# A Fourier mixer with a gated feed-forward on one core: a planner counts its stores longer, holds back some of its first loads, plans anew, and puts the last half product in another bank

## The chip, the cores and the metric

The kernel runs on one core of one Trainium2 chip. The metric is the device time of one execution in microseconds (us), the median of the executions that were timed. The names of the engines in the profile are: PE (TensorE's matrix products), PEld (its weight loads, which overlap them), DVE (VectorE), ACT (ScalarE), POOL (GpSimd), SP (SyncE, which here issues nearly all transfers; SPq is that issuing). Every engine works through its own queue of instructions in order, and waits at the first one that isn't ready.

## The reference

x has 8192 rows of 448 numbers in f32. It is normalised row by row; one branch takes the Fourier transform along the 8192 rows, column by column, a small block-diagonal complex network on each frequency, and the inverse transform; the other is a gated feed-forward with 1792 hidden units. The silu of this branch times the transform branch is added to x.

```python
def reference(x, w1, b1, w2, b2, w_gate, w_up, w_down):
    xn = layernorm(x)                      # (8192, 448), eps 1e-5
    z = rfft(xn, along the 8192 rows)      # column by column; 4 blocks of 112 columns
    h = relu(z @ w1 + b1)                  # complex, real and imaginary part apart
    y = softshrink(h @ w2 + b2, 0.01)
    s = irfft(y, along the rows)
    f = (gelu(xn @ w_gate) * (xn @ w_up)) @ w_down      # 448 -> 1792 -> 448
    return x + s * silu(f)
```

## The kernel before, in words

**Arithmetic.** An f32 product is done as three f16 products (high by high, high by low, low by high). The large products of the feed-forward are also cut in 2 by 2 blocks and done as seven block products instead of eight, with sums of blocks made on DVE, ACT and POOL before and after. In the down projection these seven are `prod2(k, ...)` (line 1402) with k from 1 to 7; they add up in PSUM banks, and `add2` (line 1421) takes a bank into an SBUF tile `left` (the partial result of that quarter), scaled.

**Stages.** The opening (`begin`, `weights`, `begin1`) loads the first rows of x, normalises them and makes the first weights. Phase 1 runs over 16 chunks of 512 rows: layer norm, the first step of the transform, whose result `ysb` is stored to `t`, and units of the feed-forward, whose results `th` are stored to `prt` for the next pass. In the same stretch the block weights are made: sums of blocks (`wst`, `cb`) are cast to a high and a low f16 part (`wo`) on ACT and DVE or POOL, stored to the scratch tensors `wsp` (gate and up) and `dsp` (down), and loaded again from there when they are wanted. Phase 2 does the small network, group by group, between the units of the feed-forward. Phase 3 (`tiles3`, line 2077) does the inverse transform tile by tile (bank `bf`), multiplies with the gate (`g`), adds x and stores the output, again between units of the feed-forward.

**Banks and rings.** PSUM is used as four rings of two banks each, which the profile names `bx`, `by`, `bd` and `bf`. SBUF buffers are rings too. A product that opens a bank waits until DVE or ACT has read what stood there.

**The planner.** The order of the instructions isn't written out. A class `Pace` (line 47) runs all stages as tasks over a clock of its own: `issue` (line 137) finds from a table of costs when an instruction could start and when it would end, and a task goes on at that planned moment; the instructions come out in the order of the planned moments. So every instruction is recorded at one line (212). The planned clock has effect on the order alone; on the chip only semaphores decide. The table `STEPS` (line 41) sets, from a planned time on, a due-time width, what a load's planned end has added to it, how free an engine must be to be given a piece of work that either of two engines can do, and a factor on ACT's, DVE's and POOL's costs. In `issue` the end of a load after 100 us has such a term, and the end of a store has none. `END3` (line 2035) is the moment up to which phase 3's tiles are spread out.

**The end of the feed-forward.** In `down2` (line 1438), the last block product (k = 4) of the very last unit is done in halves of 224 columns, both in the same bank `x` (the profile's `bd`). After each half `last_half` (line 1527) adds this half to `left`, applies silu on ACT, multiplies by the transform's result, adds x and stores.

Of the kernel before, what the change touches and what calls it, by code (L numbers as in the profile page):

```python
# [32 lines left out]
DH = D // 2  # L33
# [6 lines left out]
EPS = 1e-5  # L40
STEPS = ((0, 2.75, 0.05, 1), (100, 2.5, 0.2, 1.03), (175, 3, 0.15, 0.98), (250, 2.75, 0.05, 1), (325, 2.5, 0.05, 1), (400, 2.75, 0.05, 1.04), (475, 2.75, 0.05, 1), (550, 3.5, 0.05, 1), (700, 2.75, 0.05, 1), (775, 2.5, 0.05, 0.985), (850, 2.75, 0.05, 0.97), (925, 2.75, 0.05, 1.06), (1150, 2.5, 0.05, 0.985), (1450, 3, 0.05, 1.02), (1525, 2.75, 0.05, 0.94), )
QUIET = 200.0
# [8 lines left out]
class Pace:  # L51
# [4 lines left out]
    def __init__(self):  # L56
        self.now, self.last, self.n, self.heap = 0.0, 0.0, 0, []
        self.free, self.seen, self.dma = {"SP": 0.7, "ACT": 0.7, "DVE": 0.7, "POOL": 0.7, "PE": 1.0}, {}, 1.75
        self.port = {"DVE": [], "POOL": []}
# [77 lines left out]
    def issue(self, e, op, out, ins, run):  # L137
        outs, ins, start = self.start(e, out, ins)
        if e == "SP" or op == "dma_start":
            size = (outs or ins)[0].nbytes()  # L140
            self.dma = max(self.dma, start) + size / (320e3 if start > 10.0 else 400e3)
            if start < 10.0:
                self.free[e] = start + 0.46
                end = self.dma + 0.9
            elif op == "dma_start_transpose":
                self.free[e] = start + 1.15 + size / 380e3
                end = max(self.free[e] + 2.6, self.dma + 1.5)
            else:
                self.free[e] = start + 0.5
                end = max(start + 2.2 + size / 240e3, self.dma + 1.5) + (self.step(start)[1] if outs and start > 100.0 else 0.0)  # L150
        else:
# [248 lines left out]
def afno_geglu_kernel(ctx, tc, x, gu, wd, mlp, b1, b2, c_m, c_mt, c_small, out):  # L400
# [1004 lines left out]
    def prod2(k, p, i, h, bank_, j0, j1, first=False, last=False, halves=(0, 1)):  # L1405
        (e, c), r = PROD2[k]
        for j in range(j0, j1):
# [6 lines left out]
            for t in halves:  # L1414
                for n, (s, v) in enumerate(((0, 0), (0, 1), (1, 0))):
                    T.matmul(bank_[:, DH * t:DH * t + DH], w[s][:, 128 * t:128 * t + 128], right(7 * j + r, v),
                             start=first and j == 0 and t == 0 and n == 0,
                             stop=last and j == PF[p][1] // 2 - 1 and t == 1 and n == 2, skip_group_check=True)
            yield pe()
# [18 lines left out]
    def down2(p, i, h, last):  # L1438
# [22 lines left out]
        def tail(mid=None):  # L1461
# [19 lines left out]
            tf = yield from TH.get()  # L1481
            for t in range(2):
                yield from prod2(4, p, i, h, x, 0, n, last=True, halves=(t,))
                pace.spawn(last_half(i, QS[3], x, tf, t), pace.last)

# [40 lines left out]

    def last_half(i, qq, b, tf, a):

        v = slice(a, a + 1)
        q, s4 = EV["ptb", i, qq][:, v], blk(state["last"], *qq)[:, v]  # L1530
        x4 = EV["lgt", i, qq[0]][-1][:, v, DH * qq[1]:DH * qq[1] + DH]
        th = tf.rearrange("p (a d) -> p a d", a=2)[:, v]
        V.scalar_tensor_tensor(q, part(b, 128, 2, DH)[:, v], cB[1], q, op0=ALU.mult, op1=ALU.add)
        yield
        S.activation(th, q, AF.Silu, scale=2.0)
# [636 lines left out]
    def begin():  # L2172
# [13 lines left out]
        Q.dma_start(w[:, 0:8 * 128], gu[0][:, 0:8 * 128])  # L2186
        for a in (1, 3):
            Q.dma_start(x4[:, a, :], xv[:, a, :])
        first = []
# [12 lines left out]
        S.activation(fb[:, 4:5], mhalf[:, 0:1], AF.Gelu_apprx_tanh)  # L2202
        S.copy(identf, ident)
        banks = []
        for R in (BF, BF, BD):
# [281 lines left out]
```

## Time and profile before

| | |
|---|---|
| median of 3 executions | 1764.88 us (1763.42 to 1767.83) |
| the profiled execution | 1765.09 us, its span 1763.3 us |
| PE busy | 1744.9 us, 99% of the span |
| DVE, ACT, POOL busy | 1420.1, 1089.9, 606.7 us |
| granted TensorE clock, mean | 0.997 |
| instructions | 41411, of them 16608 matrix products |

The view of the span in 40 slices shows where PE is not full: in the first slice, the opening, and in the last.

```profile
PE   8999999999999999999999999999999999999998
DVE  7868678887888888667877877888888888788888
ACT  6557666666666765556776767667676676333334
```

Each digit is the busy share of one fortieth of the span (44 us) in tenths, and 9 stands for 90% or more. To read such a kernel, the idle time of PE is what can be won or lost, as long as the number of products stays the same; the views that name what each idle stretch of PE waited for are the ones that matter.

### The profile page before, as it was taken

To read this page: it belongs to the slowest core of one execution; us is meant where nothing else is said; L and a number is where in the kernel's file an instruction comes from. 1 tells how busy PE (TensorE), PEld (TensorE's weight loads), DVE (VectorE), ACT (ScalarE), POOL (GpSimd) and SP (SyncE) were. 2 spreads that over 40 slices of the span, in tenths; PEclk is the share of its full clock that TensorE was granted. 3 is DMA by queue.
4 is the path that set the end of the run, shared out by engine and by line. 5 is a ranking of instruction groups with operands and counts; after the bars stand their busy time and mean duration, and the time that the engine had idled before them with its cause. 6 is when DMAs were issued, how large, how long until landed. Compare 5 with 4: busy or idle time off the path is not lost.

```text
span 1763.3 us, 41411 instructions
## 1 busy us (share of the span) xinstructions
PE 1744.9 (99%) x16608; PEld 1510.6 (86%) x16608; DVE 1420.1 (81%) x2551; ACT 1089.9 (62%) x2146; POOL 606.7 (34%) x737
## 2 busy tenths in 40 slices
PE   8999999999999999999999999999999999999998
PEld 4447678899988988999999999999999999888887
DVE  7868678887888888667877877888888888788888
ACT  6557666666666765556776767667676676333334
POOL 1144333665656665311322323223322232111111
PEclk8999999999999999999999999999999999999999
DMA  6365777667575663222345744443425544999995
GB/s 239 114 169 167 224 209 216 200 182 197 152 203 184 187 193 98 73 69 75 78 148 137 188 109 109 122 107 86 112 85 122 120 93 101 271 313 306 283 313 212
DMA packets 358465, 289.44 MB, mean 164 GB/s; under 512 B 235296, under 2 KB 327200, under 8 KB 358272
## 3 DMA queue, kind: packets, MB, share of 16 engines
q1 hardware_dynamic: 358128, 286.76, 57.3%
q8 instruction: 130, 2.13, 0.5%
q14 instruction: 63, 0.52, 0.1%
q10 hardware_dynamic: 144, 0.03, 0.0%
HBM read 131.44 MB, written 106.15 MB: 135 GB/s over the span
## 4 chain that ended last, share of the span: by engine, by line
PE 92%; DVE 5%; DMA 1%; issue 1%; ACT 1%; SPq 0%; POOL 0%; DVEq 0%; ACTq 0%
PE bx L212 30%; PE by L212 24%; PE bd L212 21%; PE bf L212 17%; DVE u L212 1%; DVE gl L212 1%; DMA wsp<-wo 0%; DVE st L212 0%; DVE th L212 0%; DVE h L212 0%; DVE left L212 0%; DMA x<-in_x 0%; SPq L212 0%; DMA m<-c_m 0%; DMA wdn<-in_down 0%
## 5 line engine op out<-in xcount | busy, mean ns | idle before, releaser
L212 PEld LDWEIGHTS <-wt 128*128 128x128 f16 x9350 | 906.2, 98 | 163.0 <-issue 11.6
L212 PE MATMUL bx<-xta,wt 128*128 128x256 f16 (+1 forms) x2979 | 371.6, 276 | 0.7 <-DVE by L212 0.6
L212 PEld LDWEIGHTS <-h 128*128 128x128 f16 x2716 | 260.1, 98 | 37.1 <-issue 1.6
L212 PE MATMUL by<-xtb,wt 128*128 128x256 f16 x2080 | 256.2, 273 | 2.0 <-DVE by L212 2.0
L212 POOL TENSOR_TENSOR wt<-wt 128x256 f32<-128x256 f32 x93 | 77.2, 830 | 318.2 <-DVE wt L212 253.5
L212 PE MATMUL bd<-dw,h 128*128 128x224 f16 (+1 forms) x1272 | 172.0, 280 | 1.0 <-DVE left L212 1.0
L212 PE MATMUL by<-xta,wt 128*128 128x256 f16 (+1 forms) x1059 | 142.2, 281 | 1.2 <-ACT wt L212 0.8
L212 PE MATMUL bx<-xtb,wt 128*128 128x256 f16 x1040 | 130.5, 273 | 3.5 <-DVE v L212 3.4
L212 DVE TENSOR_TENSOR by<-bx,u 128x512 f32<-128x512 f32 x104 | 72.5, 697 | 61.8 <-PE bx L212 56.9
L212 PE MATMUL bx<-left,wt 128*128 128x256 f16 x864 | 105.1, 272 | 0.0
L212 ACT COPY u<-by 128x512 f32<-128x512 f32 x104 | 60.8, 584 | 70.0 <-PE by L212 69.6
L212 ACT ACTIVATE u<-by,fc 128x512 f32<-128x512 f32 (+1 forms) x118 | 73.4, 635 | 47.4 <-PE by L212 46.1
L212 PE MATMUL bd<-dw,wt 128*128 128x224 f16 (+1 forms) x816 | 98.9, 264 | 0.2 <-ACT th L212 0.2
L212 ACT COPY by<-bx 128x512 f32<-128x512 f32 x104 | 59.8, 575 | 52.0 <-PE bx L212 51.4
L212 ACT CAST h<-wt 128x512 f16<-128x512 f32 (+1 forms) x128 | 68.4, 536 | 33.2 <-DVE wt L212 24.8
L212 DVE TENSOR_TENSOR v<-bx,u 128x512 f32<-128x512 f32 x104 | 71.4, 686 | 20.2 <-PE bx L212 19.0
L212 PE MATMUL bd<-wt,h 128*128 128x224 f16 x696 | 84.9, 259 | 0.1
L212 PE MATMUL bf<-w2t,wn 112*128 112x112 f16 x1512 | 84.7, 213 | 0.0
L212 PEld LDWEIGHTS <-left 128*128 128x128 f16 x864 | 81.8, 98 | 1.7 <-issue 0.2
L212 DVE SCALAR_TENSOR_TENSOR left<-bd,ms,left 128x448 f32<-128x448 f32 (+1 forms) x97 | 65.1, 675 | 21.7 <-PE bd L212 20.8
L212 PEld LDWEIGHTS <-wn 112*128 112x128 f16 x1512 | 80.4, 98 | 0.9
L212 POOL TENSOR_TENSOR zs<-t,zs 112x256 f16<-112x256 f32 (+2 forms) x40 | 36.4, 909 | 124.5 <-ACT zs L212 124.4
(269 smaller groups left out, 3572.3 us busy)
## 6 DMA issues: line engine op xcount, KB each, us to landing
xts<-sx SPq DMA_DIRECT2D x32, 480.0 KB, 3.0
x<-in_x SPq DMA_DIRECT2D x17, 896.0 KB, 6.2
t<-ysb SPq DMA_DIRECT2D x64, 224.0 KB, 3.2
prt<-th SPq DMA_DIRECT2D x64, 224.0 KB, 2.5
left<-prt SPq DMA_DIRECT2D x64, 224.0 KB, 3.9
u<-t SPq DMA_DIRECT2D x32, 448.0 KB, 6.0
x<-in_x SPq DMA_DIRECT2D x32, 448.0 KB, 6.6
y<-t SPq DMA_DIRECT2D x30, 448.0 KB, 3.6
```

Source lines behind the costliest of these rows:

```text
L212: return self.pace.issue(self.name, kind, out, ins, lambda: fn(out, *args, **kw))
```

## The change

It has five parts.

1. `STEPS` is replaced: 11 entries in the place of 15, with other numbers.
2. The planner's costs change: the first transfer counts from 2.05 us in the place of 1.75, transfers of the first 10 us count at 250 KB/us in the place of 400 with 0.65 after it in the place of 0.9, and the end of every store after 100 us has 1.5 us added. Loads keep their term from `STEPS`.
3. In `begin` the loads of the second and fourth row block of x (a = 1, 3) come after a `yield 3.1`, and what follows them after a `yield 3.5`; `weights()` and `load_m(0)` are spawned at 3.15 and 3.2 in the place of 0.1 and 0.2, the tasks behind them start at 3.4 in the place of 0.3, and `begin1` at 27 in the place of 23.
4. The last block product: its first half goes to the bank `x` as before, then the whole bank is added to `left` (`add2`). Its second half opens a new bank of the ring `bx` and is added to the second half of `left` by the new function `add_half`. `last_half` waits for these and no longer adds itself.
5. All of it is planned anew, so that the order moves on every engine.

```diff
-STEPS = ((0, 2.75, 0.05, 1), (100, 2.5, 0.2, 1.03), ...
+STEPS = ((0, 2.75, 0.05, 1), (100, 3.25, 0.05, 1), (300, 2.75, 0.05, 1), (400, 3.25, 0.05, 1), ...
...
-        ... "PE": 1.0}, {}, 1.75
+        ... "PE": 1.0}, {}, 2.05
...
-            self.dma = max(self.dma, start) + size / (320e3 if start > 10.0 else 400e3)
+            self.dma = max(self.dma, start) + size / (320e3 if start > 10.0 else 250e3)
...
-                end = self.dma + 0.9
+                end = self.dma + 0.65
...
-                end = max(...) + (self.step(start)[1] if outs and start > 100.0 else 0.0)
+                end = max(...) + ((self.step(start)[1] if outs else 1.5) if start > 100.0 else 0.0)
...
     def prod2(k, p, i, h, bank_, j0, j1, first=False, last=False, halves=(0, 1)):
-                             start=first and j == 0 and t == 0 and n == 0,
-                             stop=last and j == PF[p][1] // 2 - 1 and t == 1 and n == 2, skip_group_check=True)
+                             start=first and j == 0 and t == halves[0] and n == 0,
+                             stop=last and j == PF[p][1] // 2 - 1 and t == halves[-1] and n == 2, skip_group_check=True)
...
             tf = yield from TH.get()
-            for t in range(2):
-                yield from prod2(4, p, i, h, x, 0, n, last=True, halves=(t,))
-                pace.spawn(last_half(i, QS[3], x, tf, t), pace.last)
+            yield from prod2(4, p, i, h, x, 0, n, last=True, halves=(0,))
+            e = pace.spawn(add2(p, i, QS[3], x), pace.last)
+            pace.spawn(last_half(i, QS[3], e, tf, 0), pace.last)
+            w = yield from BX.get()
+            yield from prod2(4, p, i, h, w, 0, n, first=True, last=True, halves=(1,))
+            e = pace.spawn(add_half(i, QS[3], w, 1), pace.last)
+            pace.spawn(last_half(i, QS[3], e, tf, 1), pace.last)
...
-    def last_half(i, qq, b, tf, a):
+    def add_half(i, qq, b, a):
+        v = slice(a, a + 1)
+        q = EV["ptb", i, qq][:, v]
+        V.scalar_tensor_tensor(q, part(b, 128, 2, DH)[:, v], cB[1], q, op0=ALU.mult, op1=ALU.add)
+        yield
+
+    def last_half(i, qq, e, tf, a):
+        yield e
...
-        V.scalar_tensor_tensor(q, part(b, 128, 2, DH)[:, v], cB[1], q, op0=ALU.mult, op1=ALU.add)
-        yield
...
     def begin():
...
         Q.dma_start(w[:, 0:8 * 128], gu[0][:, 0:8 * 128])
-        for a in (1, 3):
-            Q.dma_start(x4[:, a, :], xv[:, a, :])
...
         S.copy(identf, ident)
+        yield 3.1
+        for a in (1, 3):
+            Q.dma_start(x4[:, a, :], xv[:, a, :])
+        yield 3.5
...
-        pace.spawn(load_m(0), 0.2)
         pace.spawn(begin())
-        pace.spawn(weights(), 0.1)
-        yield 0.3
+        pace.spawn(weights(), 3.15)
+        pace.spawn(load_m(0), 3.2)
+        yield 3.4
...
-        pace.spawn(begin1(), 23.0)
+        pace.spawn(begin1(), 27.0)
```

Three places of the new order follow. In the rows, a name before `<-` is the tile written, those after it the tiles read, then the shape; names are those of the profile with a buffer number.

**ACT, in phase 1, where a block of gate weights is cast to `wo` for the next store to `wsp`** (about 290 us into the trace of before; `gl` and `u` are the gate's and the up projection's results, taken out of the banks `bx` and `by`). Before:

```order
L212 COPY u_3340<-by 128x512
L212 ACTIVATE wo<-wst,fc 128x256
L212 ACTIVATE wo<-wst,fc 128x512
L212 ACTIVATE x_2696<-x_2696,st 128x448
L212 ACTIVATE gl<-bx,fc 128x512
L212 ACTIVATE u_3386<-by,fc 128x512
```

Now:

```order
L212 COPY u_3347<-by 128x512
L212 ACTIVATE x_2718<-x_2718,st 128x448 x2
L212 ACTIVATE gl<-bx,fc 128x512
L212 ACTIVATE u_3390<-by,fc 128x512
L212 CAST xs<-x_2718 128x2x448
L212 CAST h<-gl 128x256
L212 ACTIVATE ysb<-bf 128x2x224
L212 COPY sf<-x_2718 128x64
L212 ACTIVATE wo<-wst,fc 128x256
L212 ACTIVATE wo<-wst,fc 128x512
```

The two casts to `wo` stood ahead of the reads of `bx` and `by`; now they stand behind both, and behind four further pieces.

**SP's queue, about 200 us into the trace of before**, around a store of down weights (`dsp<-wo`). Before:

```order
L212 DMA t<-ysb 64x1792 x2
L212 DMA prt<-th 128x448 x2
L212 DMA dsp<-wo 256x1x1568
L212 DMA wdn<-in_down 128x2x448
L212 DMA x_2174<-in_x 128x1792
```

Now:

```order
L212 DMA t<-ysb 64x1792 x2
L212 DMA dsp<-wo 256x1x1568
L212 DMA wdn<-in_down 128x2x448
L212 DMA prt<-th 128x448 x2
L212 DMA x_2161<-in_x 128x1792
```

The store of `wo` stood behind the two stores of `th`; now it is issued ahead of them.

**DVE, its last pieces** (`left` reads a bank of the feed-forward, `g` one of the inverse transform; `th` and `g` are multiplied by the transform `s` or have `x` added, and are then stored). Before:

```order
L212 SCALAR_TENSOR_TENSOR left<-bd,ms,left 128x448
L212 TENSOR_TENSOR th<-th,x_25058 128x448
L212 SCALAR_TENSOR_TENSOR left<-bd,ms,left 128x224
L212 TENSOR_TENSOR th<-th,s_21907 128x448
L212 TENSOR_TENSOR th<-th,s_21907 128x224
L212 TENSOR_TENSOR th<-th,x_24887 128x448
L212 SCALAR_TENSOR_TENSOR left<-bd,ms,left 128x224
L212 TENSOR_TENSOR th<-th,x_25058 128x224
L212 TENSOR_TENSOR th<-th,s_21907 128x224
L212 TENSOR_TENSOR th<-th,x_25058 128x224
```

Now:

```order
L212 SCALAR_TENSOR_TENSOR left<-bd,ms,left 128x448
L212 TENSOR_TENSOR th<-th,s_22066 128x448
L212 SCALAR_TENSOR_TENSOR g_25273<-bf,ms,g_25273 128x448
L212 SCALAR_TENSOR_TENSOR left<-bx,ms,left 128x224
L212 TENSOR_TENSOR th<-th,s_22066 128x224
L212 TENSOR_TENSOR th<-th,x_25118 128x448
L212 TENSOR_TENSOR th<-th,x_25118 128x224
L212 TENSOR_TENSOR th<-th,s_22066 128x224
L212 SCALAR_TENSOR_TENSOR g_25273<-bf,ms,g_25273 128x448
L212 TENSOR_TENSOR th<-th,x_25118 128x224
L212 TENSOR_TENSOR th<-th,s_22066 128x448
L212 TENSOR_TENSOR th<-th,x_24866 128x448
```

The second half is read from `bx` in the place of `bd`, and a last tile of the inverse transform (`g_25273`) now falls in between. On PE its three products into `bf` are the very last, behind the second half in `bx`; POOL's last two rows are the additions of x to this `g`.

More of the change, by code (lines that the diff above doesn't have):

```diff
@@ L40 @@
 EPS = 1e-5
-STEPS = ((0, 2.75, 0.05, 1), (100, 2.5, 0.2, 1.03), (175, 3, 0.15, 0.98), (250, 2.75, 0.05, 1), (325, 2.5, 0.05, 1), (400, 2.75, 0.05, 1.04), (475, 2.75, 0.05, 1), (550, 3.5, 0.05, 1), (700, 2.75, 0.05, 1), (775, 2.5, 0.05, 0.985), (850, 2.75, 0.05, 0.97), (925, 2.75, 0.05, 1.06), (1150, 2.5, 0.05, 0.985), (1450, 3, 0.05, 1.02), (1525, 2.75, 0.05, 0.94), )
+STEPS = ((0, 2.75, 0.05, 1), (100, 3.25, 0.05, 1), (300, 2.75, 0.05, 1), (400, 3.25, 0.05, 1), (500, 2.75, 0.3, 1), (700, 2.5, 0.05, 0.985), (800, 2.75, 0.05, 1.03), (900, 2.5, 0.05, 0.985), (1000, 2.75, 0.05, 1), (1300, 2.75, 0.05, 1.06), (1500, 2.5, 0.05, 0.985), )
 QUIET = 200.0
@@ L57, in __init__ @@
         self.now, self.last, self.n, self.heap = 0.0, 0.0, 0, []
-        self.free, self.seen, self.dma = {"SP": 0.7, "ACT": 0.7, "DVE": 0.7, "POOL": 0.7, "PE": 1.0}, {}, 1.75
+        self.free, self.seen, self.dma = {"SP": 0.7, "ACT": 0.7, "DVE": 0.7, "POOL": 0.7, "PE": 1.0}, {}, 2.05
         self.port = {"DVE": [], "POOL": []}
@@ L149, in issue @@
                 self.free[e] = start + 0.5
-                end = max(start + 2.2 + size / 240e3, self.dma + 1.5) + (self.step(start)[1] if outs and start > 100.0 else 0.0)
+                end = max(start + 2.2 + size / 240e3, self.dma + 1.5) + ((self.step(start)[1] if outs else 1.5) if start > 100.0 else 0.0)
         else:
```

## The prediction

> **What bounds the kernel now.** I read the page's table of busy times and its chain of waits first.
>
> ```profile
> PE 1744.9 (99%) x16608; PEld 1510.6 (86%) x16608; DVE 1420.1 (81%) x2551; ACT 1089.9 (62%) x2146; POOL 606.7 (34%) x737
> PE 92%; DVE 5%; DMA 1%; issue 1%; ACT 1%; SPq 0%; POOL 0%; DVEq 0%; ACTq 0%
> ```
>
> PE is busy for 1744.9 of 1763.3 us, and the chain that ended last lies on it for 92%. The change keeps the number and the sizes of PE's products (16608 in both orders), so it can only move PE's idle time. The next view cuts the span into stages and gives PE's busy time in each: the first column is the stretch, the second its length, the third PE.
>
> ```profile
> 100.00:310.00 210.00, 205.17 (x1514) 147.36 (x1513) 156.04 (x286) 133.13 (x235) 75.27 (x109) 1.00 0.72 200
> 310.00:750.00 440.00, 437.84 (x4094) 394.62 (x4092) 363.51 (x671) 286.58 (x562) 250.48 (x316) 1.00 0.59 167
> 750.00:1650.00 900.00, 900.00 (x9553) 828.07 (x9551) 726.96 (x1270) 565.35 (x1146) 238.03 (x246) 1.00 0.52 140
> 1650.00:1757.20 107.20, 106.41 (x978) 94.43 (x977) 91.29 (x153) 41.94 (x73) 18.71 (x21) 1.00 0.87 276
> 1757.20:1763.30 6.10, 1.02 (x9) 0.77 (x8) 3.29 (x9) 0.96 (x3) 0.00 (x0) 0.95 0.37 127
> ```
>
> Length less busy gives PE's idle time: 4.83 us in the first row, 2.16, 0 and 0.79 in the next three, 5.08 in the last: 7.78 us over 1657 us of steady work, and a tail. That is small beside 1765 us, so this change can move the time by a few us either way. About 0.3% (5.3 us) is what a measurement of this kernel can tell from no change: the three runs shown lie up to 4.4 us apart. The band around the median is 1759.6 to 1770.2. The view of PE's waits names what the idle time waited for (us in all, times, longest), and that of the waits for DMA what stood behind it:
>
> ```profile
> PE bx L212 <- DVE v L212: 3.4, 2, 2.3
> PE bd L212 <- ACT xs L212: 2.9, 1, 2.9
> PE by L212 <- DVE by L212: 2.0, 2, 1.0
> PE bx L212 <- DVE gl L212: 1.4, 1, 1.4
> ACT wo L212 <- DMA wsp<-wo: 4.6, 2, 4.4
> ACT wo L212 <- DMA dsp<-wo: 1.9, 1, 1.9
> ```
>
> The longest is 2.3 us, and ACT waits there for a store, 4.4 us long. A store's end is what the change counts longer.
>
> **The store stall near 290 us.** The rows of the timeline (start, us, engine, operation, and in brackets the idle time ahead with its releaser):
>
> ```profile
> 288.10 0.36 SPq L212 DMA_DIRECT2D wsp<-wo  x1
> 295.71 1.12 ACT L212 ACTIVATE wo<-wst,fc 128x256 f16<-128x256 f32 x2 [4.36 <-DMA wsp<-wo]
> 297.39 0.67 ACT L212 ACTIVATE gl<-bx,fc 128x512 f32<-128x512 f32 x1
> 298.76 0.68 DVE L212 TENSOR_TENSOR v<-bx,u 128x512 f32<-128x512 f32 x1
> 299.49 1.25 PE L212 MATMUL bx<-xtb,wt 128*128 128x256 f16 x10 [2.30 <-DVE v L212]
> 306.00 0.88 PEld L212 LDWEIGHTS <-h 128*128 128x128 f16 x10 [0.40 <-DVE h L212]
> ```
>
> ACT wants to write `wo` again while the store of the old content is under way: issued at 288.10, let go just ahead of 295.71, 7.6 us. Behind it in ACT's queue stands `gl<-bx`, behind that DVE's `v<-bx`, and PE waits 2.30 us for that bank; a late `h` costs 0.40 more. In the new order both casts to `wo` stand behind `x` (twice), `gl<-bx`, `u<-by`, `xs`, `h`, `ysb` and `sf`. ACT was free for its wait at 295.71 - 4.36 = 291.35. The rows ahead of the casts now cost:
>
> ```profile
> 208.91 0.76 ACT L212 ACTIVATE x<-x,st 128x448 f32<-128x448 f32 x1
> L212 ACT ACTIVATE u<-by,fc 128x512 f32<-128x512 f32 (+1 forms) x118 | 73.4, 635 | 47.4 <-PE by L212 46.1
> 211.30 0.94 ACT L212 CAST xs<-x 128x896 f16<-128x896 f32 x1
> ```
>
> Two `x` of 0.76, `gl` 0.67, `u` 0.64 and `xs` 0.94 are 3.8 us, and with `h`, `ysb` and `sf`, taken at 1 us together as an estimate from the shapes of these rows, 4.8: ACT comes to `wo` at 296.2 or later, behind the landing. And if the store is still late, the bank reads are already done. So the 2.30 and the 0.40 go, **-2.7 us**; both ends: 0 if the store is itself issued 2 us later or more, -2.7 otherwise.
>
> **The store stall near 209 us** is alike, with a store to `dsp`:
>
> ```profile
> 201.42 1.40 SPq L212 DMA_DIRECT2D prt<-th  x2
> 202.91 0.56 SPq L212 DMA_DIRECT2D dsp<-wo x1
> 208.62 0.38 ACT L212 CAST wo<-wst 128x224 f16<-128x224 f32 x1 [1.85 <-DMA dsp<-wo]
> 210.92 1.25 PE L212 MATMUL by<-xtb,wt 128*128 128x256 f16 x10 [1.04 <-DVE by L212]
> ```
>
> ACT waits 1.85 us for it; `u<-by` and DVE's `by` are queued behind it, and PE waits 1.04. The store now goes ahead of the two `prt<-th`, which keep SP's queue for 1.40 us and wait for `th`. With 1.40 of the 1.85 gone, 0.45 is left on ACT, less than the 1.85 - 1.04 = 0.81 that the work already queued on PE covers. **-1.0 us**; the other end is 0.
>
> **The rest of the idle time** in phase 1, phase 2 and 3 is 7.78 - 2.3 - 0.4 - 1.0 = 4.1 us, in places where DVE or ACT comes a little late at a bank; all orders have them, and planning anew draws them afresh. The view of waits shows two more `bx` waits, of 1.1 (the other of 3.4) and 1.4 us. In the stretch of the first, POOL no longer stands beside DVE in the new order; I take -0.8 for it and +0.5 for places that I can't see, **-0.3** together. The bounds: -3.6, were nearly all to vanish, and +4, were they to double.
>
> **The opening.** ACT and PE wait there for rows of x:
>
> ```profile
> 8.18 0.58 ACT L212 ACTIVATE xs<-x 128x448 f16<-128x448 f32 x1 [4.09 <-DMA x<-in_x]
> 8.96 0.59 PE L212 MATMUL bd<-identf,fx 128*2 128x128 f32 x2 [2.87 <-ACT xs L212]
> ```
>
> Loads that were really held back would come on top of the 4.09. But in the new order SP's first 18 rows are the same ones in the same sequence, the loads of x and of weights among them, and on the other engines nothing differs until PE's row 406, where the opening is all but over: a planned moment is no wait on the chip. **0 us**, with -0.8 to +0.3 (one group of ACT's work changes places behind that) as the ends.
>
> **The tail.** At the end DVE is the engine to watch:
>
> ```profile
> 1756.09 0.68 DVE L212 SCALAR_TENSOR_TENSOR left<-bd,ms,left 128x448 f32<-128x448 f32 x1
> 1756.69 0.61 DVE L212 TENSOR_TENSOR th<-th,x 128x448 f32<-128x448 f32 x1
> 1757.22 0.45 DVE L212 SCALAR_TENSOR_TENSOR left<-bd,ms,left 128x224 f32<-128x224 f32 x1
> 1757.71 0.73 PE L212 MATMUL bd<-dw,h 128*128 128x224 f16 x6 [0.96 <-DVE left L212]
> 1758.96 0.45 DVE L212 SCALAR_TENSOR_TENSOR left<-bd,ms,left 128x224 f32<-128x224 f32 x1
> 1759.32 0.38 DVE L212 TENSOR_TENSOR th<-th,x 128x224 f32<-128x224 f32 x1
> 1760.29 0.39 DVE L212 TENSOR_TENSOR th<-th,x 128x224 f32<-128x224 f32 x1
> out<-th SPq DMA_DIRECT2D x2, 112.0 KB, 1.7
> ```
>
> Before, PE's second half waits 0.96 us until DVE has read the first out of the same bank. A bank of its own takes this wait away: PE ends about 1 us sooner, near 1757.7 in the place of 1758.74 (1758.29 + 0.45). But the end is set by DVE and a store. Before, DVE's last piece ends at 1760.68 (1760.29 + 0.39); a half store takes 1.7, so it lands at 1762.4, and the span ends 0.9 later.
>
> Now count the new order. Back to back, pitches in the rows above are 0.60 (448 from a bank: 1756.69 - 1756.09), 0.53 (448 in SBUF), 0.36 (224 from a bank) and, as an estimate, 0.31 (224 in SBUF, 0.39 less the same overlap of 0.08). The twelve rows that stand at DVE's end begin when the first half is in `bd`. Behind that PE has the second half (nine products of 224) and six products of 448 into `bf`. From the rows above, six of 224 take 0.58 (1757.71 to 1758.29), so nine take 0.87; one of 448 is two of 224, so six take 1.16. These 2.0 us ahead of 1757.7 put DVE's start near 1755.7. The twelve are three of 448 from a bank (1.80), four of 448 in SBUF (2.12), one of 224 from a bank (0.36) and four of 224 in SBUF (1.24): 5.5 us, so DVE ends near 1761.2. The last store is of two halves, 224 KB; I estimate 2.1 us for it (1.7 and 0.4 for twice the bytes), and with 0.9 behind it the span ends at 1764.2, **+0.9** against 1763.3.
>
> That is the lower end, since POOL now adds x to the last `g` twice in this stretch. What that does stands earlier in the trace:
>
> ```profile
> 1674.58 1.44 POOL L212 TENSOR_TENSOR g<-g,x 128x448 f32<-128x448 f32 x1 [3.19 <-DVE g L212]
> 1674.95 1.55 DVE L212 SCALAR_TENSOR_TENSOR th<-th,left 128x448 f32<-128x448 f32 x1
> ```
>
> Beside POOL's addition the DVE piece, with both inputs in SBUF, takes 1.55 us, where its like (1756.69) takes 0.61: about 0.95 more, and the POOL piece itself grows too. The first addition comes while DVE reads a bank, the second while DVE goes through SBUF pieces back to back; each can hold DVE for up to 1.44. I take 1.1 each, between 0.95 and 1.44, **+3.1 us** for the tail in all, with +0.9 and +3.8 as the ends. The Trainium skill (SBUF — State Buffer, section "SBUF: two separate sides") says why such a pair collides: DVE and GpSimd share one pair of ports, taken as an exclusive lock for a whole instruction, by GpSimd's pieces and by DVE's pieces with two SBUF inputs. The trace agrees, with 1.55 beside 0.61; by that rule the tail costs +3.1, and without it +0.9.
>
> **The sum:** -2.7 - 1.0 - 0.3 + 0 + 3.1 = -0.9 us. The profiled execution took 1765.09 us, 0.2 over the median of 1764.88, so the forecast is 1764.2 by the one and **1763.9 us** by the median, which I take.
>
> **Rivals.** *The stalls at stores come again elsewhere (slower).* The same mechanism has 13 places, six stores to `wsp` and seven to `dsp`, each with a cast to `wo` waiting for it; here it decides whenever a cast stands ahead of bank reads and its store lands later than the planner thinks. The store above took 7.6 us, and 1.5 us more in the plan may not cover it when transfers are dense, since the DMA engines are busy 72% of the time in that stage (the second last column above). For it speaks that the plan's other stores were as blind before and two of 13 hit; against it that the two places I followed are clear now. With two such places, 2.3 and 0.4 each, the gain of 3.7 is all but given back: 1763.9 + 5.4 - 0.5 = about 1768.8; with three 1771.5. From two places on it is slower than before.
>
> *The tail is free and the rest shrinks (faster).* If POOL's additions fall between DVE's pieces, the tail costs +0.9, and if the rest loses 2 us more, the sum is -2.7 - 1.0 - 2.3 + 0.9 = -5.1: 1759.8. For it speaks that DVE reads banks, which need no lock by the row above, for four of the twelve; against it that POOL's second addition meets four SBUF pieces in a row.
>
> *The loads do hold back.* If ACT's sums waited 1 us longer than 4.09, PE's 2.87 would grow by as much: 1764.9. The equal queue speaks against it.
>
> **Chances.** The forecast 0.48 (its own range 1760.5 to 1767), stalls elsewhere 0.27, the free tail with a shrinking rest 0.21, real holding 0.04. Faster by over 0.3% (under 1759.6) comes from about half of the free-tail case and a quarter of the forecast's (the rest's bound of -3.6): 0.11 + 0.12, with 0.01 over, 0.24. Slower (over 1770.2) is some 0.6 of the stalls case and a little of the others (the bound of +4): 0.20. Within the band 0.56. The range for 8 in 10 reaches half-way into both cases: 1758.8 to 1769.5.
>
> **What would show it.** In the changed trace: ACT's waits for `wsp<-wo` and `dsp<-wo` of 4.4 and 1.9 us gone or not ahead of a bank read, and PE's waits of 2.30 and 1.04 with them; PE's idle time from 100 to 310 us near 1.1 in the place of 4.83; the first 24 us unchanged, with 4.09 on ACT and 2.87 on PE; no wait of PE ahead of its second half; DVE ending 2 to 3 us behind its old moment, with at least one SBUF piece over 1.2 us beside POOL's `g`. I am wrong if PE's idle time beyond 310 us is over 6 us or under 1, or if PE's start of full work moves by over 1 us.

## The result and the profile after

The changed kernel takes **1770.83 us** (median of 6 executions, 1768.61 to 1773.1). The kernel before, run beside it, takes 1763.8 us. The ratio is 1.0037, with an interval of 1.0027 to 1.0048: slower, by 7 us. The forecast was 1763.9, with a range up to 1769.5. The profiled execution of the changed kernel took 1773.1 us, span 1771.3, which is 2.3 over its median and the slowest of the six; the one of before took 1765.09 with span 1763.3, 1.3 over its median. Two of the twelve executions of `storelate` below ran at a granted clock of 0.61 and 0.65 and took 2760 and 2597 us; its time is the median of the other ten.

The page of the changed kernel, busy times of the engines:

```profile
PE 1746.1 (99%) x16608; PEld 1510.9 (85%) x16608; DVE 1412.6 (80%) x2533; ACT 1088.9 (61%) x2146; POOL 620.7 (35%) x755
```

PE does the same products for 1746.1 us in the place of 1744.9. The span grew by 8.0 us, so 6.8 of it is idle time. The stages of the changed kernel (stretch, length, PE's busy time, then PEld, DVE, ACT, POOL, the granted clock, DMA share, GB/s):

```profile
100.00:310.00 210.00, 206.66 (x1535) 149.52 (x1533) 156.06 (x276) 134.11 (x239) 84.04 (x116) 1.00 0.73 205
310.00:750.00 440.00, 433.92 (x4034) 390.23 (x4032) 364.52 (x673) 282.22 (x548) 229.65 (x297) 1.00 0.58 165
...
1475.00:1650.00 175.00, 174.13 (x1659) 156.53 (x1656) 139.41 (x233) 72.51 (x135) 40.13 (x46) 1.00 0.89 262
1650.00:1762.80 112.80, 111.47 (x1014) 97.68 (x1011) 92.52 (x151) 42.97 (x75) 26.78 (x30) 1.00 0.89 280
1762.80:1771.30 8.50, 0.00 (x1) 0.00 (x0) 5.44 (x9) 0.85 (x2) 2.27 (x2) 0.72 0.38 135
```

Length less busy is PE's idle time. From 100 to 310 us it fell, from 4.83 to 3.34. From 310 to 750 us it rose, from 2.16 to 6.08: +3.9. From 1475 to 1650 us it is 0.87, where it was 0; that one wait isn't part of every execution, since `oldtail` and `nolock` below, with the same order up to there, show none and `tailv` one of 0.43. PE's last product ends at 1762.80 in the place of 1758.74, and behind it the span goes on for 8.5 us in the place of 4.6: +3.9. What PE waited for:

```profile
PE bx L212 <- DVE v L212: 3.9, 5, 2.2
PE bd L212 <- ACT xs L212: 2.4, 1, 2.4
PE bx L212 <- ACT by L212: 1.2, 1, 1.2
...
PE bx L212 <- ACT th L212: 0.9, 1, 0.9
```

The wait of 2.30 us behind the store near 290 us is gone. But there is a new one of 2.2, also for `v`, and many small ones. The new one stands in the timeline of the changed kernel near 571 us:

```profile
566.73 2.15 POOL L212 TENSOR_TENSOR xs<-x,xs 128x896 f16<-128x896 f32 x1 [1.81 <-ACT xs L212]
567.58 1.58 DVE L212 TENSOR_TENSOR gl<-gl 128x256 f32<-128x256 f32 x1
568.84 1.82 POOL L212 TENSOR_TENSOR sx<-sf,sx 128x768 f16<-128x768 f32 x1
569.08 1.78 DVE L212 TENSOR_TENSOR sf<-x,sf 128x192 f32<-128x192 f32 x1
570.79 0.68 DVE L212 TENSOR_TENSOR v<-bx,u 128x512 f32<-128x512 f32 x1
571.52 1.95 PE L212 MATMUL bx<-xtb,wt 128*128 128x256 f16 x10 [2.19 <-DVE v L212]
```

Two small pieces of DVE, both with SBUF inputs alone, take 1.58 and 1.78 us while a long subtraction runs on POOL beside each. `v`, which empties PE's bank, stands behind them. No store has a part in it. In this execution the wait cost more than its 2.19 us, because the granted clock (the third number from the end) was low behind it:

```profile
571.90:575.40 3.50, 3.50 (x20) 2.70 (x19) 3.22 (x7) 1.33 (x3) 1.24 (x2) 0.51 1.18 259
```

The ten products into `bx` take 1.95 us, where ten take 1.26 in the view of experiment 4, and the twelve into `bd` behind them 2.33, where twelve take 1.31 in `earlytile`: 1.7 us in all. The profiled executions of `oldtail`, `tailv` and `earlytile` have the same wait (2.19 to 2.20) and the full clock behind it, so this part belongs to the execution.

Near 594 us a piece of DVE of 4 columns takes 1.82 us in the same manner:

```profile
591.99 1.88 POOL L212 TENSOR_TENSOR wo<-cb,wo 128x896 f16<-128x896 f32 x1
592.08 1.82 DVE L212 SCALAR_TENSOR_TENSOR st<-st 128x4 f32<-128x4 f32 x1 [2.06 <-POOL st L212]
593.82 1.26 DVE L212 SCALAR_TENSOR_TENSOR th<-bd,ms,th 128x448 f32<-128x448 f32 x2
594.54 1.31 PE L212 MATMUL bd<-dw,h 128*128 128x224 f16 x12 [0.69 <-DVE th L212]
```

And the tail of the changed kernel:

```profile
1760.85 0.68 DVE L212 SCALAR_TENSOR_TENSOR left<-bd,ms,left 128x448 f32<-128x448 f32 x1
1762.07 0.73 PE L212 MATMUL bf<-u,mt 128*128 128x448 f16 x3
1762.73 1.13 POOL L212 TENSOR_TENSOR g<-g,x 128x448 f32<-128x448 f32 x1 [11.81 <-DVE g L212]
1762.93 1.18 DVE L212 TENSOR_TENSOR th<-th,s 128x224 f32<-128x224 f32 x1
1765.93 1.20 POOL L212 TENSOR_TENSOR g<-g,x 128x448 f32<-128x448 f32 x1 [2.06 <-DVE g L212]
1766.07 1.54 DVE L212 TENSOR_TENSOR th<-th,s 128x448 f32<-128x448 f32 x1
```

PE doesn't wait ahead of its second half any more. DVE starts on its last twelve pieces at 1760.85 and ends at 1768.27, 7.4 us later. 1.7 of them were lost beside POOL's two additions (1.18 and 1.54 in the place of 0.38 and 0.62).

### The profile page after: what moved, and what is told of

Read it like the earlier page. It is cut to its first block, busy times and chain, and to the rows that moved or that the text cites. A ratio compares the mean times of both kernels' runs of the same rounds, so it can differ in the third digit from the quotient of the medians.

```text
span 1771.3 us, 41437 instructions
## 1 busy us (share of the span) xinstructions
PE 1746.1 (99%) x16608; PEld 1510.9 (85%) x16608; DVE 1412.6 (80%) x2533; ACT 1088.9 (61%) x2146; POOL 620.7 (35%) x755
## 4 chain that ended last, share of the span: by engine, by line
PE 90%; DVE 5%; issue 1%; DMA 1%; ACT 1%; POOL 1%; SPq 0%; DVEq 0%; ACTq 0%; POOLq 0%
PE bx L212 29%; PE by L212 24%; PE bd L212 21%; PE bf L212 16%; DVE wt L212 1%; DVE left L212 1%; DVE u L212 0%; DVE h L212 0%; DMA g<-gsp 0%; DMA left<-prt 0%; DVE gl L212 0%; SPq L212 0%; DMA x<-in_x 0%; DVE th L212 0%; DVE st L212 0%
## 5 line engine op out<-in xcount | busy, mean ns | idle before, releaser
L212 POOL TENSOR_TENSOR wt<-wt 128x256 f32<-128x256 f32 x87 | 71.2, 818 | 225.8 <-DVE wt L212 197.7
L212 POOL TENSOR_TENSOR zs<-t,zs 112x256 f16<-112x256 f32 (+1 forms) x46 | 40.7, 885 | 187.4 <-ACT zs L212 170.4
L212 DVE SCALAR_TENSOR_TENSOR left<-bd,ms,left 128x448 f32<-128x448 f32 x96 | 64.4, 679 | 26.8 <-PE bd L212 26.0
```

What stands on the lines that cost most here:

```text
L212: return self.pace.issue(self.name, kind, out, ins, lambda: fn(out, *args, **kw))
```

## The experiments

The changed kernel is called the new order here, the kernel before the old order. Most experiments keep one of the two and change a few instructions at their place: the planner goes on counting as it did, and only what is emitted differs, so that nothing else moves. "Tail" is the time from the end of PE's last product to the end of the span, in the profiled execution: 4.57 us in the old order, 8.51 in the new.

**1. The new order with the old bank** (`oldtail`). Part 4 of the change is undone.

```diff
-            yield from prod2(4, p, i, h, x, 0, n, last=True, halves=(0,))
-            e = pace.spawn(add2(p, i, QS[3], x), pace.last)
...
-            w = yield from BX.get()
-            yield from prod2(4, p, i, h, w, 0, n, first=True, last=True, halves=(1,))
...
+            for t in range(2):
+                yield from prod2(4, p, i, h, x, 0, n, last=True, halves=(t,))
+                pace.spawn(last_half(i, QS[3], x, tf, t), pace.last)
```

> The changed kernel with only the last half product as it was (both halves in one bank); everything ahead of the last 20 us stays in the same order. Theory: the tail is long because a last tile of the inverse transform stands among DVE's last twelve pieces and POOL's additions hold DVE, not because of the bank. Then PE waits about 1 us again ahead of its second half, but the end is set by DVE's 7.4 us of work behind its first reading, so the median stays at 1770.8 (1770.3 to 1771.8), and the time from PE's end to the span's end shrinks from 8.6 to about 7.6 us. Rival: the new bank costs the time itself (the reading of the whole bank, one piece more of DVE); then 2 us or more come back: 1768.8 or less.

1771.07 us (1769.36 to 1771.45): the same as the new order. The tail is 8.53. The expected wait of PE didn't come back, nor did the tail get shorter: three products into `bf` now stand between the two halves and cover DVE's reading. So in the new order the bank is worth nothing, either way.

**2. The old order with the new bank** (`newtail`). Part 4 alone.

> The kernel before with only the last half product changed; the order ahead of the last 20 us stays. Theory (the bank is harmless and takes PE's wait of 0.96 away, DVE reads 224 columns more, 0.24): 0.3 to 1.0 us faster than before, 1762.8 to 1763.5, PE's wait of 0.96 gone and the time from PE's end to the span's end up from 4.6 to about 5.2. Rival (the bank costs): slower by 1 us or more, 1764.8 or above.

1764.41 us (1761.77 to 1766.18), ratio 0.9997 with an interval of 0.9988 to 1.0006: no change that can be told, and not the gain that I had expected. PE's wait of 0.96 is gone and its last product ends at 1757.65, 1.09 us sooner. But the tail grows from 4.57 to 5.70 and DVE ends at 1760.69, where it ended at 1760.68. The wait was covered: DVE and its stores set the end, and they start no sooner. The bank is harmless and useless; the rival falls too.

**3. POOL's last two additions on DVE** (`tailv`), in the new order. Here and in 4, 11 and 12, `n` counts POOL's instructions in the order of the plan.

```diff
+                if n in (749, 750):          # POOL's last two instructions
+                    run = lambda: getattr(self.pace.vector, op)(out, *args, **kw)
```

> The changed kernel with POOL's last two additions (x to the last g) on DVE at the same places of the order. Theory (a lock between POOL and DVE): DVE's two pieces of 1.18 and 1.54 us fall to 0.38 and 0.62, and two of 0.53 to 0.6 come in: the time from PE's end to the span's end goes from 8.6 to about 8.0, the median to about 1770.2. Rival (no lock; DVE was late for another reason): the two pieces stay long and the time grows by 1.1 us, 1771.9.

1770.23 us (1769.06 to 1771.85), 0.6 below the new order, which the medians can't tell from no change, and a tail of 8.24. Two rows of its tail beside those above:

```profile
1758.80 0.38 DVE L212 TENSOR_TENSOR th<-th,s 128x224 f32<-128x224 f32 x1
1761.67 0.62 DVE L212 TENSOR_TENSOR th<-th,s 128x448 f32<-128x448 f32 x1
```

The two long pieces are short again, 0.38 and 0.62: POOL had held them, for 0.80 and 0.92 us. But DVE now does the additions itself, so DVE's stretch shrinks from 7.42 to 6.65 us only (1756.71 to 1763.36). POOL's additions are worth 0.3 to 0.8 us of the tail, net of doing them elsewhere. The rest I put down to the whole tile of the inverse transform that stands there; this run doesn't show it, and experiment 9 bears on it.

**4. Four of POOL's subtractions as fills with zeros** (`nolock`), in the new order; the low parts are left out.

```diff
+                if n in (274, 353, 354, 375):
+                    run = lambda: self.engine.memset(out, 0.0)
```

> The changed kernel with four of POOL's subtractions (the low parts of sx near 460 us, of xs and sx near 567 us, of wo near 592 us) replaced by a fill with zeros at the same places; this leaves these low parts out. The order stays. Theory (the new waits of PE from 310 to 750 us come from POOL holding DVE's SBUF pieces): DVE's pieces of 1.84, 1.58, 1.78 and 1.82 us fall to 0.2 to 0.7, PE's waits of 2.19 (571 us), 0.70 (463 us) and 0.69 (594 us) go, and the median falls by 3.0 to 3.6 us to 1767.2 to 1767.8. Rival (DVE simply has too much of its own to do there): at most 0.7 us less, 1770.1 or above, and the wait near 571 us stays over 1.5.

1766.77 us (1765.78 to 1768.16): 4.1 us below the new order. PE's idle time from 310 to 750 us falls from 6.08 to 3.35, by 2.7; the intervals of the two kernels are 3 to 4 us wide and can't tell 4.1 from 2.7. The place near 571 us, now:

```profile
567.23 0.41 DVE L212 TENSOR_TENSOR gl<-gl 128x256 f32<-128x256 f32 x1
567.57 0.34 DVE L212 TENSOR_TENSOR sf<-x,sf 128x192 f32<-128x192 f32 x1
567.84 0.68 DVE L212 TENSOR_TENSOR v<-bx,u 128x512 f32<-128x512 f32 x1
568.82 1.26 PE L212 MATMUL bx<-xtb,wt 128*128 128x256 f16 x10
```

DVE's two pieces take 0.41 and 0.34 us, and PE doesn't wait. The waits near 463 and 594 us are gone as well; a new one of 0.9 us near 566 us came instead of part of them. The theory holds: POOL's long pieces held DVE, and DVE held PE.

**5. The store near 290 us, in the old order** (`storelate`). ACT's two casts to `wo`, DVE's two pieces behind them and ACT's scaling of `wst` are emitted behind the next `h` (`n` counts all instructions here):

```diff
+            if n in (2900, 2912, 2926, 2928, 2953):
+                held.append(run)
+                run = lambda: None
+            elif n == 2956:
+                run = lambda: (fn(out, *args, **kw), [h() for h in held])
```

> The kernel before with one edit near 290 us: the two casts to wo, DVE's two pieces behind them and the scaling of wst are issued behind the reads of bx and by and the next h; all else stays in order. Theory (PE waits there only because ACT waits for the store with the bank reads behind it): PE's wait of 2.30 to 2.9 us and the 0.40 behind it go, and the median falls by 2 to 2.7 us to 1762 to 1762.6. Rival (the late store makes something else late instead: wo itself, its product, or cb): PE waits at another place within 30 us, and the gain is under 1 us.

1763.59 us (1761.02 to 1766.39), ratio 0.9995 with an interval of 0.9986 to 1.0004: no gain that can be told. The rival was right. The timeline of that kernel:

```profile
296.57 1.25 PE L212 MATMUL bx<-xtb,wt 128*128 128x256 f16 x10
296.65 1.12 ACT L212 ACTIVATE wo<-wst,fc 128x256 f16<-128x256 f32 x2 [1.61 <-DMA wsp<-wo]
300.10 0.94 ACT L212 CAST xs<-x 128x896 f16<-128x896 f32 x1
302.29 1.55 DVE L212 TENSOR_TENSOR xs<-x,xs 128x896 f16<-128x896 f32 x1
303.90 0.54 PE L212 MATMUL bf<-xs,m 128*128 128x448 f16 x2 [2.45 <-DVE xs L212]
```

PE no longer waits for `v` at 296.57, where it had waited 2.30 us. Seven us on it waits 2.45 us for `xs`: ACT is still held by the store for 1.61 us, and `xs`, behind it in ACT's queue, is as late as before: DVE's piece starts at 302.29, and at 302.34 in the old order. ACT and DVE, not one bank read, were behind there. In the new order the casts stand behind `xs` as well, and from 290 to 310 us PE of the changed kernel waits for nothing.

**6 to 8. One part of the change alone, on the old kernel, planned anew**: the stores' 1.5 us (`bstores`), the table (`bsteps`), the opening with its costs (`bopen`). The diffs are those of the change, part by part.

> The kernel before with only the stores counted 1.5 us longer. Theory (a plan drawn anew puts PE's waits at other places by chance, wherever POOL and DVE meet): the store wait near 290 us may shrink, but PE's idle time from 310 to 750 us changes by some us in either direction; 1762 to 1769. Rival (longer stores help as meant): 1761 or less, with no wait of PE behind a store.

> The kernel before with only the new table STEPS. Theory: drawn anew as well, 1764 to 1770; no wait of PE behind a store near 290 us is promised. Rival (the table is what makes the changed kernel slow, by its 0.3 from 500 to 700 us, which lets work go to a busy engine): the same waits behind POOL's locks between 500 and 700 us as in the changed kernel, 3 us or more over before in that stretch, 1768 or above.

> The kernel before with only the new costs and waits of the opening (parts 2 and 3 but the stores). Theory: the first 24 us keep their times within 0.5 us on the same clock, since the transfers stand in the same order; what comes behind is drawn anew, 1762 to 1769. Rival (the loads are held back on the chip): ACT's wait for x of 4.1 us grows by 0.5 us or more and PE's first product on it comes later than 9.4 us.

| | median, us | ratio to before, interval |
|---|---|---|
| stores 1.5 us longer alone | 1850.11 | 1.0493 (1.0479 to 1.0507) |
| the table alone | 1796.73 | 1.0191 (1.0176 to 1.0206) |
| the opening alone | 1773.01 | 1.0054 (1.0042 to 1.0066) |

Each part alone is slower than all of them together, and by more than my theory had allowed for any of them. Where it goes with the stores alone (PE's waits):

```profile
PE bf L212 <- DVE g L212: 24.6, 13, 10.8
PE bf L212 <- DMA mt<-c_mt: 14.7, 2, 10.9
```

Nearly all of these lie behind 1750 us, where PE is idle for 59 us in all; and its products take 13.5 us more over the whole span (1758.4 in the place of 1744.9), with a granted clock of 0.60 from 1750 us to PE's end. There the units of the feed-forward have run out, and tiles of the inverse transform follow each other with nothing between them, each waiting for its loads and stores. The table alone has the same picture at smaller size. I read this as a table that is fitted to the costs: with the costs of before or of after, each with its own table, the last tiles end about where the units end, and with a mixture they don't. The rival on the table has the right side (1768 or above) but not the place: of the 32 us, PE's idle time from 310 to 750 us has 5.2 (7.39 in the place of 2.16), and most of the rest lies behind 1750 us. From 500 to 700 us, where the rival had looked for 3 us or more, it is 4.04 in the place of 1.77, and the two longest waits from 310 to 750 us (2.5 and 1.9) are for loads (`xta`), not behind POOL. `bopen`, with the old table, has 3.66 from 500 to 700 us, so such idle time comes without the new table too. `bopen` answers the question of the opening: its first rows are below, in the points.

**9. Another order from 1480 us of the plan on** (`earlytile`), in the new order. The table's last factor is 1.02 and stores count no longer there:

```diff
-(1500, 2.5, 0.05, 0.985), )
+(1500, 2.5, 0.05, 1.02), )
...
-((self.step(start)[1] if outs else 1.5) if start > 100.0 else 0.0)
+((self.step(start)[1] if outs else 1.5 if start < 1480.0 else 0.0) if start > 100.0 else 0.0)
```

> The changed kernel with another order from 1480 us of the plan on alone (stores count no longer than before there, and the last factor of the table is 1.02 in the place of 0.985): the last tile of the inverse transform now stands well ahead of the last half product, and POOL adds no g in the last 5 us. The order ahead of that is the changed kernel's. Theory (the tail is long because that tile is last): the time from PE's end to the span's end falls from 8.5 to about 5.7, as in the kernel before with the new bank, and the median by 2.5 to 3.5 us to 1767.3 to 1768.3. Rival (the tail is only a shift; DVE's work is the same in sum and PE waits for it earlier): PE's idle time from 1650 us on grows by 2 us or more, and the median stays at 1770.

1766.56 us (1762.78 to 1768.1): 4.3 us below the new order, more than expected. The rows of the timeline with PE's last product and DVE's last pieces:

```profile
1756.43 0.45 PE L212 MATMUL bx<-wt,h 128*128 128x224 f16 x3
...
1758.69 1.22 DVE L212 TENSOR_TENSOR th<-th,x 128x448 f32<-128x448 f32 x3
```

PE ends at 1756.88 and the span at 1763.0: a tail of 6.13 in the place of 8.51. From 1650 us to PE's end PE has no idle time, where the new order has 1.33 (and `oldtail`, `tailv` and `nolock`, with the same order there, have it too). So 2.4 us are from the tail and 1.3 from these small waits, 3.7 of the 4.3. The edit draws everything behind 1480 us of the plan anew: it shows what this end of the order costs, and not what the last tile alone does.

**10 and 11. Both causes together** (`earlynolock`, with the fills; `earlymove`, with the same four subtractions moved from POOL to DVE, nothing left out).

> The same, with the four fills with zeros in the place of POOL's subtractions from 460 to 592 us as well; these four low parts are left out. Theory (two causes that add up, the tail's tile and POOL's locks): 1763.3 to 1764.5, level with the kernel before. Rival (the two overlap): 1766 or above.

> As the one before the last, with the four subtractions moved from POOL to DVE at the same places (nothing is left out). Theory: DVE no longer waits for POOL (1.28 to 1.65 us each) but does them itself (0.9 to 1.1 us each): PE's waits near 571, 463 and 594 us shrink by half, 1.0 to 2.0 us gained on that kernel, 1766 to 1767. Rival (DVE full): no gain, 1767.5 or above.

1762.95 us (1761.68 to 1765.57) and 1762.96 us (1761.59 to 1764.17), ratios to before 0.9994 (0.9985 to 1.0003) and 0.9994 (0.9985 to 1.0002). The two causes add up: 4.3 for the tail's order and 3.6 for the four pieces bring the new order from 1770.83 to the time of the kernel before. Moving the pieces to DVE does as much as leaving them out, twice what I had expected. PE's wait near 570 us, 2.19 in the new order, is 0.59 in `earlymove`.

**12. One subtraction from POOL to DVE in the old order** (`bmove`).

```diff
+                if n in (394,):              # wo, 128x896, near 624 us
+                    run = lambda: getattr(self.pace.vector, op)(out, *args, **kw)
```

> The kernel before with one subtraction (wo, 128x896, near 624 us) moved from POOL to DVE, where it stands behind v. Theory (the wait of 1.10 us of PE near 627 us comes from POOL holding DVE's gl for 1.3 us): that wait goes and comes back for at most 0.3 us, 0.8 to 1.1 us faster than before, 1763.2 to 1763.6, too little to tell in the median but plain in PE's waits. Rival (DVE's own work is the cause): the wait stays near 1 us or comes back within 10 us.

1762.43 us (1759.06 to 1764.51), ratio 0.9990 with an interval of 0.9981 to 0.9999, which only just leaves out 1: about 0.1% faster than before. The trace says more than the median. The place in the kernel before:

```profile
624.01 1.88 POOL L212 TENSOR_TENSOR wo<-cb,wo 128x896 f16<-128x896 f32 x1
624.44 1.74 DVE L212 TENSOR_TENSOR gl<-gl 128x256 f32<-128x256 f32 x1
626.83 1.25 PE L212 MATMUL bx<-xtb,wt 128*128 128x256 f16 x10 [1.10 <-DVE v L212]
```

And in `bmove`:

```profile
623.40 0.39 DVE L212 TENSOR_TENSOR gl<-gl 128x256 f32<-128x256 f32 x1
623.71 0.68 DVE L212 TENSOR_TENSOR v<-bx,u 128x512 f32<-128x512 f32 x1
624.52 1.25 PE L212 MATMUL bx<-xtb,wt 128*128 128x256 f16 x10
625.76 1.40 DVE L216 TENSOR_TENSOR wo<-cb,wo 128x896 f16<-128x896 f32 x1
```

`gl` takes 0.39 us (1.74 in the kernel before), PE doesn't wait, and its idle time from 310 to 750 us falls from 2.16 to 0.85 us. Its median is the lowest of all these kernels, by less than the runs can tell. Both kernels of the case have such places.

PE's idle time by stage, from the same view of each kernel's profiled execution (length less busy, us):

| | old order | new order | nolock | earlytile | earlymove | bmove |
|---|---|---|---|---|---|---|
| 100 to 310 | 4.83 | 3.34 | 2.85 | 2.14 | 3.50 | 5.21 |
| 310 to 750 | 2.16 | 6.08 | 3.35 | 6.11 | 3.10 | 0.85 |
| 1475 to 1650 | 0 | 0.87 | 0 | 0 | 0 | 0 |
| 1650 to PE's end | 1.30 | 1.33 | 1.33 | 0 | 0 | 1.31 |
| tail | 4.57 | 8.51 | 8.49 | 6.13 | 6.12 | 4.58 |
| median | 1763.8 | 1770.83 | 1766.77 | 1766.56 | 1762.96 | 1762.43 |

## Why the prediction was wrong, point by point

**What bounds the kernel** was right in the main: PE's idle time and the tail moved. That the change "can only move PE's idle time" was too strong: behind the wait at 571 us the same products took 1.7 us more in the profiled execution, at a granted clock of 0.51.

**The store stall near 290 us** ("so the 2.30 and the 0.40 go, -2.7 us"). In the new order they did go: no wait of ACT for `wsp<-wo` is left. (The 0.40 was the weight load's wait; PE's products show no idle time over 0.15 us there, so the term was a little large from the start.) But the stage from 100 to 310 us lost 1.5 us of idle time in the profiled execution and about 2.7 in `earlytile`'s, not the 3.7 of both store terms. One new wait of 0.9 us (for `th`, near 148 us) took part of it. Experiment 5 shows that the step was weaker than I wrote: in the old order, taking the wait away at its place moved it 7 us on. I had asked what is queued behind the waiting cast, and not what else is late on that engine once the cast goes.

**The store stall near 209 us** ("-1.0 us; the other end is 0"). It was exchanged for another. With the store of `wo` ahead, the stores of `th` come later, and the timeline of the new order shows the next `th` late:

```profile
199.14 0.55 SPq L212 DMA_DIRECT2D dsp<-wo  x1
200.53 2.03 SPq L212 DMA_DIRECT2D prt<-th  x2
206.90 0.63 ACT L212 ACTIVATE th<-bd,ms 128x448 f32<-128x448 f32 x1 [4.23 <-PE by L212]
207.44 0.59 ACT L212 COPY by<-bx 128x512 f32<-128x512 f32 x1
```

PE then waits 1.18 us for `by`, which is ACT's copy at 207.44. The row names PE as the releaser, but the bank `bd` was ready long before; the first of the two stores landed at 206.82 by the trace, just ahead of ACT's start, so I read the wait as one for the store. I didn't test that. It isn't in every execution: of the kernels that share this order up to there, it is in `nolock`, `earlymove` and `earlynolock`, and not in `oldtail`, `tailv` and `earlytile`.

**The rest of the idle time** ("-0.8 for it and +0.5 for places that I can't see, -0.3 together"). This is the step that failed. It became +3.9 us from 310 to 750 us, which is the upper bound of +4 that I had set for all stages, and some 1.9 more behind 1475 us (0.87 up to 1650, which not every execution has, and 1.0 behind, where before's 0.96 of the tail went and other waits came). In all PE is idle for 8.3 us between 310 us and its end, over the 6 that I had named as a sign of being wrong. I had seen one place of the kind, near 627 us, and counted it as a gain, since POOL's piece there was gone from the new order. I didn't look for POOL's long pieces next to DVE's short ones at all the other places, though the order shows both. Experiments 4, 10 and 11 show that 3.6 to 4.1 us of the loss by the medians, 2.7 to 3.0 of it seen as idle time from 310 to 750 us, hang on four of POOL's pieces. A fifth place of the kind was left as it was: near 618 us a subtraction on POOL takes 1.99 us, DVE's `sf` beside it 1.79, and PE waits 0.94 for what DVE reads next; that this wait hangs on POOL too isn't tested. It isn't that POOL held DVE much more in all. Adding up, over DVE's pieces from 310 to 750 us, what each took beyond the 20th percentile of its like (same instruction, tiles and shape) gives 56.7 us in the old order and 57.8 in the new. Where they fall decides: in the new order more of them fall just ahead of a piece that PE waits for.

**The opening** ("0 us") was right, and the rival that the loads are held back is out. ACT's wait for x and PE's behind it, in `bopen`:

```profile
7.91 0.58 ACT L212 ACTIVATE xs<-x 128x448 f16<-128x448 f32 x1 [3.97 <-DMA x<-in_x]
8.71 0.38 PE L212 MATMUL bd<-identf,fx 128*2 128x128 f32 x2 [2.04 <-ACT xs L212]
```

They are 3.97 and 2.04 here, 4.00 and 2.44 in the changed kernel, and 4.09 and 2.87 before. PE's full work did start 1.4 us sooner in the profile of the changed kernel (its product number 301 at 62.15 us, before at 63.54), over the 1 us that I had named as a sign of being wrong. That goes with the clock and not with the order: the granted clock of the first 24 us is 0.79 in the kernel before and 0.86 in the changed one, but also 0.79 in `oldtail`, which has the new opening, and 0.86 in `newtail`, which has the old one, and there the product starts at 64.08 and 62.07.

**The tail** ("+3.1 us", bounds +0.9 to +3.8) was right in its size: from PE's end to the span's end +3.9, less the 0.96 that PE no longer waits, +3.0. Its make-up was off a little: I gave 2.2 of it to POOL's lock, and the two held pieces lost 1.7; the work without the lock then came to 1.3 in the place of 0.9. Moving the additions wins only 0.3 to 0.8 (experiment 3), since DVE has to do them instead. The Trainium skill (SBUF — State Buffer, section "SBUF: two separate sides") limits the lock of a DVE piece with two SBUF inputs to GpSimd pieces that read SBUF. The runs agree: in experiment 4 a fill on POOL stands beside DVE's `st` of 4 columns, which takes 0.17 us, where it took 1.82 beside the subtraction.

```profile
587.60 0.84 POOL L218 MEMSET wo<- 128x896 f16 x1
587.71 0.17 DVE L212 SCALAR_TENSOR_TENSOR st<-st 128x4 f32<-128x4 f32 x1 [2.07 <-POOL st L212]
```

**The rivals.** "The stalls at stores come again elsewhere" had the right sign and a right amount (1768.8 to 1771.5) for a wrong reason: the largest stalls that came are behind POOL, not behind stores, so its amount was luck. "The tail is free" fell. No rival had POOL's lock in the middle of the kernel, although I used the same lock for the tail.

**The sum**, in the profiled executions: 100 to 310 us -1.5, 310 to 750 us +3.9, 1475 us to PE's end +0.9 (with the 0.96 that went), the tail +3.9, the opening's idle time -0.4, PE's own products +1.2 (near -1.0 in the opening and +1.7 behind 571 us, both by the granted clock, and 0.5 besides); together +8.0, the difference of the spans. The medians differ by 7.0.

What stays open: why the new plan puts POOL's pieces at worse places. The planner knows of the shared port in its costs, so it places them where its own clock has no collision; whether the chip's times differ from that clock by enough to undo this, no run tests.

## What to carry to other kernels

When an order is drawn anew, its gains at the places that the edit aimed at can be the smaller part, as here. Go through the new order for the known hazards at every place (here: a long POOL piece with SBUF operands ahead of a short DVE piece that a bank waits for), not only at the places that were bad before, and take the bound for "the rest" from the number of such places, not from the sum of the waits that happen to show now. A table that was fitted to one set of costs can't be judged with another: three parts of this change, each alone, cost 9 to 86 us.

A wait that ends at a late engine goes on to that engine's next customer when the first one is served. Before a removed wait is counted as a gain, look at what else stands behind it in the queue.

## What the runs showed of the hardware that I had not expected

A DVE piece of 4 columns that takes 0.17 us beside a fill took 1.82 us beside a POOL subtraction of 1.88 us that had started 0.09 us ahead of it: the price of the collision is what is left of POOL's piece, whatever the length of DVE's. The whole trace of the kernel before says the same. 119 of DVE's pieces take over 0.4 us more than the 20th percentile of their like; all of them begin while a POOL piece runs, and for the middle half of them the excess is what is left of that piece, less 0.13 to 0.14 us. In the changed kernel it is 133 of 135, and the other two begin within 0.01 us of a POOL piece. Moving the four long pieces to DVE cost nothing that could be seen, though DVE is busy for 80% of the span: 1762.96 us with them there, 1762.95 without them.

Behind a wait of PE of about 2.2 us or more the granted clock was half for 3.4 us in some profiled executions (the changed kernel behind 2.19 us, `storelate` behind 2.45, `newtail` behind 2.94) and full in others (the kernel before behind 2.30, `bmove` behind 2.59, and `oldtail`, `tailv` and `earlytile` behind 2.19 to 2.20). What decides it these runs don't show.
